# Twelve rows of each wo head on five DMA engines, instruction blocks aligned on three engines, x issued behind wq

## The chip, the cores and the metric

The kernel runs on one core of a Trainium2 chip. A core has TensorE (PE, with its weight loads as PEld), VectorE (DVE), ScalarE (ACT), GpSimd (POOL) and SyncE (SP), and 16 DMA engines. The metric is the device time of one execution in microseconds (us); lower is better.

## The reference

One decoding step of attention with grouped heads over a sliding window of the cache, with both projections. In bfloat16:

```python
B, Sq, D = 32, 1, 512
Hq, Hkv, Sk, Dh = 32, 8, 2048, 128
W = min(4096, max(256, Sk // 4))             # 512: the last 512 positions
rep = Hq // Hkv                              # 4
q = (x @ wq).reshape(B, Sq, Hq, Dh).transpose(0, 2, 1, 3)
k = repeat(k_cache[:, :, Sk - W:, :], rep, axis=1)
v = repeat(v_cache[:, :, Sk - W:, :], rep, axis=1)
p = softmax(einsum("bhqd,bhkd->bhqk", q, k) * Dh ** -0.5)
o = einsum("bhqk,bhkd->bhqd", p, v)
return o.transpose(0, 2, 1, 3).reshape(B, Sq, Hq * Dh) @ wo
```

wq is 512 x 4096 and wo 4096 x 512 (4 MB each); the windows of the two caches are 32 MB each.

## The kernel before

**Stages.** x (32 x 512) is transposed on PE by a selection matrix (L325), copied to SBUF by DVE (L453), and multiplied with wq (L336: 8 groups of 4 matmuls, copied out by DVE and ACT in turn). DVE transposes q to `QT_sb` (L483), and POOL builds from it the block-diagonal `QBD` (L312), one batch quarter at a time. Then come eight rounds q = 0 to 7 of four batch rows each, with these steps (a letter is a step in the written orders below):

- K, V (SP, L248 and L255): load the round's K and V rows, 4 MB each; later V's in two pieces;
- T (DVE, L491): transpose half of K into `KT_sb[:, w]`; S (PE, L353): scores of that half;
- M (DVE): maximum, X (ACT): exponential and sum, N (DVE): normalising;
- E (PE, L368): probabilities to the rows of V, with the selection matrices `E_sb`; G (ACT): copy out;
- B (DVE and ACT): spread over heads by a mask into `bd`; P (PE, L383): times V, 32 groups;
- C (DVE and ACT): pick the wanted blocks into `C_sb`;
- F and D (PE L395, ACT L561): fold the first 4 x NI values of each head with `F_sb` into `o_sel`; H and U (PE L404, ACT L566): fold the last NX values with `F_ext` into `o_ext`.

At the end PE multiplies with wo in three pieces W0, W1, W2 (L421) and with the extra rows (L435), two copies take the two halves out (DVE L524, ACT L582), and SP and ACT store them (L233).

**How wo is laid out.** A head has 128 rows of wo, 1 KB each. Rows 0 to 4 x NI - 1 go to 128 partitions (32 heads x 4 groups of NI rows), in pieces `WOP` of those NI rows (L269); NI is 30, so 120 rows of a head. The last NX = 128 - 4 NI = 8 rows of each head go to a tile of 64 partitions, one head on a partition, by four small loads, `HEADS` (L262). They reuse the memory of `QT_sb`, which ACT first fills with zeros (step Z0, L572, after POOL has made its last `QBD`).

**Orders.** Each compute engine runs a written list of steps (`PE_OPS`, `DVE_OPS`, `ACT_OPS`); `needs` says which other steps each waits for. SP issues the loads in the order of `LOADS`, waiting in order, so a load stands behind every load written ahead of it. x's three loads are issued by ACT (L204), wq by SP (L208), ahead of the rest. POOL builds constants at the start, among them the four shifted copies of `E_sb` (L301); DVE makes `F_sb` (L471) and `F_ext` (L474). `pe.addr_align(256, offset=178)` places PE's code: its next instruction is loaded 178 slots past a boundary of 256 instruction slots. The other engines' code is not placed.

Of the kernel before, what the change touches and what calls it, by code (L numbers as in the profile page):

```python
# [5 lines left out]
BF16 = mybir.dt.bfloat16  # L6
# [14 lines left out]
P2.12.32 F2 H2 S4.0 S4.1 P3.0.12 E4 P3.12.32 S5.0 S5.1 S6.0 P4.0.4 E5 P4.4.8 S6.1 P4.8.24 E6 P4.24.32  # L21
F3 H3 S7.0 P5.0.20 S7.1 P5.20.32 E7 F4 H4 P6.0.32 F5 H5 P7.0.32 F6 H6 F7 H7
"""
# [6 lines left out]
X0 X1 G0 B0.4.8 G1 B1.4.8 C0.0.4 D0 U0 X2 G2 B2.4.8 C1.0.4 D1 U1 X3 G3 B3.4.8 C2.0.4 D2 U2 X4 G4 B4.4.8  # L30
C3.0.2 X5 G5 B5.4.8 X6 G6 C4.0.2 B6.4.7 D3 U3 B6.7.8 Z0 X7 C5.0.2 G7 B7.5.6 D4 U4 B7.6.8 C6.0.2 D5 U5 C7.0.2
D6 U6 D7 U7
"""
# [6 lines left out]
V_PIECES = 5 * [[0, 32]] + 2 * [[0, 16, 32]] + [[0, 18, 32]]  # L40
WOP = [(0, 20), (20, 28), (28, 30)]
HEADS = [(0, 20, 4, 0), (20, 25, 1, 32), (25, 30, 1, 33), (30, 32, 1, 34)]
# [6 lines left out]
def bass_standalone__sliding_block_cached__sampling_kernel(  # L49
# [8 lines left out]
    B, Sq, D = x.shape  # L58
# [11 lines left out]
    R = W // KB  # L70
    NI = 30
    NX = DH - 4 * NI
# [57 lines left out]
    with ExitStack() as es:  # L130
# [17 lines left out]
        F_ext = sb("F_ext", [P, 64], F32)  # L148
        E_sb = sb("E_sb", [P, KB, REP, 32, KB], BF16)
        F_sb = sb("F_sb", [P, 4, HQ, 4], F32)  # L150
# [8 lines left out]
        wo_sb = K_sb[0][:, 0:NI * D].rearrange("p (i n) -> p i n", i=NI)  # L159
        wx_row = QT_sb[0:64].rearrange("p j w h t -> p (j w h t)")  # L160
        wx_sb = wx_row.rearrange("p (i n) -> p i n", i=NX)
# [17 lines left out]
        def folds(q):  # L179
# [10 lines left out]
            "pe_xT pe_q pe_Y dve_xT dve_q dve_QT dve_m dve_r dve_c act_q act_warm out_y "  # L190
            "pool_x pool_e pool_ei pool_q pool_f pool_m pool_j pool_qbd pool_fz"
        ).split()
# [9 lines left out]

        for b0, b1 in X_PARTS:
            nc.scalar.dma_start(  # L204
                x_sb[b0:b1, :], x[b0:b1].rearrange("b s d -> b (s d)")
            ).then_inc(sem_x, 16)

        nc.sync.dma_start(  # L208
            V_sb[1][:, :], wq.rearrange("(p k) n -> p (k n)", k=DKT)
        ).then_inc(sem_wq, 16)  # L210
        regions = es.enter_context(ExitStack())
        block = regions.enter_context(nc.Block())
# [25 lines left out]
        @block.sync  # L238
        def _(sp):
            wait = Waits(sp)  # L240
            wo_h = wo.rearrange("(h r) n -> h (r n)", r=DH)
            wo_r = wo_h[:, 0:4 * NI * D].rearrange("h (d m) -> h d m", d=4)
            for op in ops_of(" ".join(LOADS)):
                kind, q = op[0], op[1]
                if kind == "K":
                    if q >= 2:
                        wait([ends["T", q - 2, 1]])
                    sp.dma_start(K_sb[q % 2][:, :], rows(k_cache, q)).then_inc(sem_k[q % 2], 16)  # L248
                elif kind == "V":
                    if q == 1:  # L250
                        sp.wait_ge(s["pe_q"], 8)
                    r0, r1 = (4 * g for g in V_PIECES[q][op[2]:op[2] + 2])
                    if q >= 2:
                        wait([ends["P", q - 2, r1 // 4 - 1]])
                    sp.dma_start(  # L255
                        V_sb[q % 2][:, r0 * DH:r1 * DH], rows(v_cache, q, r0, r1)
                    ).then_inc(sem_v[q % 2][op[2]], 16)
                elif kind == "A":
                    wait([ends["Z", 0]])
                    h0, h1, k, p0 = HEADS[q]  # L260
                    n = (h1 - h0) // k
                    sp.dma_start(  # L262
                        wx_row[p0:p0 + 4 * n:1 if k == 4 else 4, :],
                        wo_h[h0:h1, 4 * NI * D:].rearrange("(k j) m -> j k m", k=k),
                    ).then_inc(sem_wx, 16)
                else:
                    wait([ends["T", NQ - 2, 1]])
                    i0, i1 = WOP[q]
                    sp.dma_start(  # L269
                        wo_sb[:, i0:i1, :].rearrange("p i n -> p (i n)"),  # L270
                        wo_r[:, :, i0 * D:i1 * D],
                    ).then_inc(sem_wo[q], 16)
            store(sp, 0)

        @block.gpsimd
        def _(pool):
            wait = Waits(pool)

            def diag(t, pattern, name):
# [16 lines left out]
                 [[-1, REP], [-4, 4], [-16, HKV]], "pool_ei")  # L296
            pool.memset(E_sb[:, :, :, :, :], 0.0).then_inc(s["pool_e"], 1)
            pool.wait_ge(s["pool_e"], 1)
            pool.wait_ge(s["pool_ei"], 2)
            for k in range(KB):  # L300
                pool.tensor_copy(E_sb[:, k, :, :, k], E_id[:, :, :]).then_inc(s["pool_e"], 1)  # L301
            pool.wait_ge(s["pool_e"], 5)
            pool.wait_ge(s["pool_q"], 1)
            pool.wait_ge(s["dve_QT"], 1)
            for q in range(NQ):
                if q >= 2:
                    wait([ends["S", q - 2, 1]])
                for b in range(4):
                    pr = slice(32 * b, 32 * b + 32)
                    if q or b:  # L310
# [4 lines left out]
                        QT_sb[pr, q].rearrange("p w (h e) t -> p w t h e", h=HKV),  # L315
                    ).then_inc(s["pool_qbd"], 1)

        @block.tensor
        def _(pe):
            pe.addr_align(256, offset=178)  # L320
            wait = Waits(pe)
# [41 lines left out]
            def to_value_rows(q):  # L363
                if q == 0:
                    pe.wait_ge(s["pool_e"], 5)
                for e in range(REP):
                    for k in range(KB):
                        ins = pe.matmul(  # L368
                            EP_ps[:, e * R:(e + 1) * R],
                            lhsT=E_sb[:, k, e].rearrange("p m j -> p (m j)"),  # L370
                            rhs=P_bf[:, k * R:(k + 1) * R],
                            start=k == 0, stop=k == KB - 1, tile_position=(0, 0),
                        )
                return ins
# [16 lines left out]
            def fold(q):  # L391
                if q == 0:
                    pe.wait_ge(s["dve_c"], 7 + len(HEADS))
                for d in range(4):
# [15 lines left out]
            for op in orders["PE"]:  # L410
                wait(needs(op))
                run[op[0]](*op[1:]).then_inc(op_sem["PE", op[0]], 1)
            wait([ends["D", NQ - 1]])
            for j, (i0, i1) in enumerate(WOP):
                pe.wait_ge(sem_wo[j], 16)
                last = j == len(WOP) - 1
                for cs in ((0, 1), (2, 3)) if last else (range(4),):
                    for i in range(i0, i1):
                        for c in cs:
                            n = 2 * (c % 2) + c // 2  # L420
                            ins = pe.matmul(  # L421
                                Y_ps[32 * c:32 * (c + 1), 0:P],
                                lhsT=o_sel[:, i, :],
                                rhs=wo_sb[:, i, n * P:(n + 1) * P],
                                start=i == 0, stop=i == NI - 1, tile_position=(0, 32 * c),
                            )
                    if last:
                        ins.then_inc(s["pe_Y"], 1)
                if j == 0:
                    wait([ends["U", NQ - 1]])  # L430
                    pe.wait_ge(sem_wx, 16 * len(HEADS))
                    for i in range(NX):
                        for c in range(4):
                            n = 2 * (c % 2) + c // 2
                            pe.matmul(  # L435
                                Y_ps[32 * c:32 * (c + 1), 0:P],
                                lhsT=o_ext[:, i, :],
                                rhs=wx_sb[:, i, n * P:(n + 1) * P],
                                start=False, stop=False, tile_position=(0, 32 * c),
                            )  # L440

# [8 lines left out]
        def _(dve):  # L450
# [14 lines left out]
            dve.wait_ge(s["dve_c"], 2)  # L465
            dve.wait_ge(s["pool_fz"], 2)
            dve.tensor_reduce(
                mask[:, :], m_red[:, :].rearrange("p (h k) -> p h k", h=HKV), AX.X, ALU.add
            ).then_inc(s["dve_c"], 1)
            for d in range(4):  # L470
                dve.tensor_copy(F_sb[:, d, :, d], F_hd[:, :]).then_inc(s["dve_c"], 1)  # L471
            for h0, h1, k, p0 in HEADS:
                n = (h1 - h0) // k
                dve.tensor_copy(  # L474
                    F_ext[:, p0:p0 + 4 * n].rearrange("p (j k) -> p k j", k=4)[:, 0:k],
                    F_hd[:, h0:h1].rearrange("p (k j) -> p k j", k=k),
                ).then_inc(s["dve_c"], 1)
            for n in range(4):
# [48 lines left out]
        def _(act):  # L527
# [41 lines left out]

            def zero(_):  # L570
                act.wait_ge(s["pool_qbd"], 4 * NQ)
                return act.activation(  # L572
                    wx_row, junk[0:64, 0:1].to_broadcast([64, NX * D]), ACTF.Copy
                )

            run = {"X": exponential, "G": gather, "B": spread, "C": pick, "D": folded,
                   "U": folded_ext, "Z": zero}
            for op in orders["ACT"]:
# [36 lines left out]
```

## Time and profile before

| | |
|---|---|
| median of 3 runs | 184.42 us (184.26 to 184.52) |
| the profiled execution | 184.59 us |
| its span, first to last instruction | 183.3 us |
| mean granted clock of TensorE | 0.842 |
| busy: PE, DVE, ACT, POOL | 120.4, 106.7, 54.2, 17.1 us |
| moved by DMA | 75.80 MB, mean 414 GB/s |

The profile is of one execution. Busy times are of one engine each and overlap. In the chain of waits a line "SPq" is SyncE issuing a transfer, and "DMA a<-b" the time from an issue to the landing that ended a wait. The landing of a transfer is that of its last DMA engine.

### The profile page before, as it was taken

To read this page: it belongs to the slowest core of one execution; us is meant where nothing else is said; L and a number is where in the kernel's file an instruction comes from. 1 tells how busy PE (TensorE), PEld (TensorE's weight loads), DVE (VectorE), ACT (ScalarE), POOL (GpSimd) and SP (SyncE) were. 2 spreads that over 40 slices of the span, in tenths; PEclk is the share of its full clock that TensorE was granted. 3 is DMA by queue.
4 is the path that set the end of the run, shared out by engine and by line. 5 is a ranking of instruction groups with operands and counts; after the bars stand their busy time and mean duration, and the time that the engine had idled before them with its cause. 6 is when DMAs were issued, how large, how long until landed. Compare 5 with 4: busy or idle time off the path is not lost.

```text
span 183.3 us, 3870 instructions
## 1 busy us (share of the span) xinstructions
PE 120.4 (66%) x1676; PEld 58.0 (32%) x1676; DVE 106.7 (58%) x109; ACT 54.2 (30%) x101; POOL 17.1 (9%) x53
## 2 busy tenths in 40 slices
PE   0029802416779699429944995440799978999984
PEld 0013300002535344304520252000255433655463
DVE  0042399998569534973289326999825994703030
ACT  3001300010590527501650135001053693803040
POOL 7900013020200020002000200001000000000000
PEclk9999995555769999996995599655559999999999
DMA  6998999989999999999999999999999999999981
GB/s 234 459 443 386 429 458 454 422 386 451 458 443 383 429 454 447 415 401 451 442 429 415 424 442 440 408 429 451 436 408 404 426 426 429 432 418 427 436 359 62
DMA packets 3517, 75.80 MB, mean 414 GB/s; under 512 B 429, under 2 KB 525, under 8 KB 653
## 3 DMA queue, kind: packets, MB, share of 16 engines
q1 hardware_dynamic: 3409, 75.52, 96.5%
q8 instruction: 13, 0.21, 0.5%
q10 hardware_dynamic: 92, 0.05, 0.1%
q14 instruction: 3, 0.02, 0.0%
HBM read 75.53 MB, written 0.03 MB: 412 GB/s over the span
## 4 chain that ended last, share of the span: by engine, by line
DMA 65%; DVE 19%; PE 8%; issue 4%; SPq 3%; ACT 0%; DVEq 0%
DMA K_sb<-in_k_cache_dram 32%; DVE KT_sb L491 16%; DMA V_sb<-in_v_cache_dram 16%; DMA K_sb<-in_wo_dram 11%; DMA V_sb<-in_wq_dram 7%; PE ps L336 5%; PE ps L383 2%; DVE QT_sb L483 2%; SPq L262 2%; SPq L255 1%; PE ps L421 1%; PE ps L353 1%; DVE C_sb L516 0%; SPq L269 0%; ACT KT_sb L533 0%
## 5 line engine op out<-in xcount | busy, mean ns | idle before, releaser
L491 DVE STREAM_TRANSPOSE KT_sb<-K_sb 128x4096 f32<-128x4096 f32 x16 | 70.5, 4430 | 7.2 <-DMA K_sb<-in_k_cache_dram 7.1
L383 PE MATMUL ps<-V_sb,bd 32*128 32x512 bf16 x1024 | 64.0, 402 | 4.4 <-DMA V_sb<-in_v_cache_dram 2.1
L353 PE MATMUL ps<-KT_sb,QBD 128*32 128x512 bf16 x256 | 24.7, 522 | 35.2 <-DVE KT_sb L491 26.0
L383 PEld LDWEIGHTS ps<-V_sb,bd 32*128 32x128 bf16 x1024 | 27.7, 98 | 37.8 <-issue 14.1
L353 PEld LDWEIGHTS ps<-KT_sb,QBD 128*32 128x32 bf16 x256 | 6.4, 111 | 50.4 <-DVE KT_sb L491 31.3
L539 ACT ACTIVATE P_f<-ps,negmax 128x512 f32<-128x512 f32 x8 | 5.5, 687 | 56.8 <-DVE negmax L499 56.8
L557 ACT ACTIVATE C_sb<-ps 32x512 f32<-32x512 f32 x22 | 12.9, 588 | 24.4 <-PE ps L383 24.2
L552 ACT ACTIVATE bd<-PTc,mask 128x512 bf16<-128x512 bf16 x31 | 20.1, 712 | 0.3
L312 POOL COPY QBD<-QT_sb 32x128 bf16<-32x128 bf16 x32 | 9.3, 289 | 106.3 <-PE ps L353 87.2
L511 DVE TENSOR_SCALAR bd<-PTc,mask 128x512 bf16<-128x512 bf16 x33 | 9.4, 349 | 14.0 <-ACT PTc L546 14.0
L516 DVE COPY C_sb<-ps 32x512 f32<-32x512 f32 x10 | 6.9, 693 | 13.9 <-PE ps L383 13.8
L395 PE MATMUL ps<-C_sb,F_sb 128*128 128x120 f32 x64 | 9.2, 286 | 6.8 <-ACT C_sb L557 6.5
L497 DVE TENSOR_REDUCE maxv<-ps 128x1 f32<-128x512 f32 x8 | 5.5, 687 | 10.8 <-PE ps L353 10.7
L395 PEld LDWEIGHTS ps<-C_sb,F_sb 128*128 128x128 f32 x64 | 7.7, 191 | 9.6 <-ACT C_sb L557 8.4
L368 PE MATMUL ps<-P_bf,E_sb 128*128 128x128 bf16 x128 | 9.9, 239 | 1.0 <-DVE P_bf L505 1.0
L336 PE MATMUL ps<-V_sb,bd 128*128 128x512 bf16 x32 | 9.0, 451 | 2.0 <-DMA V_sb<-in_wq_dram 2.0
L546 ACT ACTIVATE PTc<-ps 128x512 bf16<-128x512 f32 x8 | 4.7, 593 | 18.3 <-PE ps L368 18.3
L368 PEld LDWEIGHTS ps<-P_bf,E_sb 128*128 128x128 bf16 x128 | 8.4, 108 | 4.9 <-DVE P_bf L505 2.8
L325 PE MATMUL ps<-bd 32*128 32x128 bf16 x4 | 0.6, 298 | 10.5 <-DMA bd<-in_x_dram 10.5
L533 ACT ACTIVATE KT_sb<-ps 128x512 bf16<-128x512 f32 x4 | 2.4, 597 | 17.0 <-PE ps L336 17.0
L453 DVE CAST bd<-ps 128x512 bf16<-128x512 f32 x1 | 0.7, 692 | 11.2 <-PE ps L325 11.2
L480 DVE CAST KT_sb<-ps 128x512 bf16<-128x512 f32 x4 | 2.8, 692 | 6.0 <-PE ps L336 6.0
(37 smaller groups left out, 44.1 us busy)
## 6 DMA issues: line engine op xcount, KB each, us to landing
K_sb<-in_k_cache_dram SPq DMA_DIRECT2D x8, 4096.0 KB, 24.6
V_sb<-in_v_cache_dram SPq DMA_DIRECT2D x5, 4096.0 KB, 28.7
V_sb<-in_v_cache_dram SPq DMA_DIRECT2D x4, 2048.0 KB, 20.6
V_sb<-in_wq_dram SPq DMA_DIRECT2D x1, 4096.0 KB, 12.3
K_sb<-in_wo_dram SPq DMA_DIRECT2D x1, 2560.0 KB, 17.6
V_sb<-in_v_cache_dram SPq DMA_DIRECT2D x1, 2304.0 KB, 14.2
V_sb<-in_v_cache_dram SPq DMA_DIRECT2D x1, 1792.0 KB, 14.9
K_sb<-in_wo_dram SPq DMA_DIRECT2D x1, 1024.0 KB, 19.4
```

Source lines behind the costliest of these rows:

```text
L312: pool.tensor_copy(QBD[pr, q % 2].rearrange("p (w t) (h c) -> p w t h c", w=2, h=HKV)[:, :, :, :, 4 * b:4 * b + 4], QT_sb[pr, q].rearrange ...
L336: ins = pe.matmul(ps[:, n], lhsT=xT_sb[:, kt, :], rhs=wq_sb[:, kt, n * 512:(n + 1) * 512], start=kt == 0, stop=kt == DKT - 1, tile_positio ...
L353: ins = pe.matmul(S_ps[32 * c:32 * c + 32, :], lhsT=QBD[:, q % 2, 2 * w + t, c0:c0 + 32], rhs=KT_sb[:, w, :, KB * h:KB * h + KB, t], start ...
L368: ins = pe.matmul(EP_ps[:, e * R:(e + 1) * R], lhsT=E_sb[:, k, e].rearrange("p m j -> p (m j)"), rhs=P_bf[:, k * R:(k + 1) * R], start=k = ...
L383: ins = pe.matmul(O_ps[:, b, :], lhsT=bd[pr, q % 2, 4 * g:4 * g + 4].rearrange("p r h e -> p (r h e)"), rhs=V_sb[q % 2][pr, 512 * g:512 * ...
L395: ins = pe.matmul(folds(q), lhsT=F_sb[:, d].rearrange("p h d -> p (h d)"), rhs=C_sb[:, q % 2, :, NI * d:NI * d + NI], start=d == 0, stop=d ...
L491: return dve.transpose(KT_sb[:, w].bitcast(F32).rearrange("p r c t -> p r (c t)"), K_sb[q % 2][:, :].bitcast(F32).rearrange("p (r w c) -> ...
L497: dve.tensor_reduce(maxv[:, q:q + 1], S_ps, AX.X, ALU.max).then_inc(s["dve_m"], 1)
L511: ins = dve.tensor_scalar(o, i, m, None, op0=ALU.mult)
L516: ins = dve.tensor_copy(*pick_args(q, r))
L552: ins = act.activation(o, i, ACTF.Copy, scale=m)
L557: ins = act.activation(*pick_args(q, r), ACTF.Copy)
```

## The change

1. NI goes from 30 to 29: wo's three pieces hold 19, 8 and 2 rows instead of 20, 8 and 2, and each head's last 12 rows, instead of 8, go by the four small loads. Their tile moves from `QT_sb` to the memory of `KT_sb[0:64, 0]`; POOL zeroes it after S7.0, in place of ACT's Z0.
2. DVE, ACT and POOL get `addr_align(128, offset=0, max_nops=0)` ahead of their work; PE's offset goes from 178 to 154.
3. x's three loads are issued by SP behind wq, not by ACT.
4. Small work moves: the copies to `F_sb` and `F_ext` go from DVE to POOL; `E_sb` becomes one padded matrix for each of the four heads of a group, of which E takes a shifted window, so three of its four copies go.
5. At the end the extra rows' matmuls come first, ahead of W0; H7 comes ahead of F7, U6 ahead of D6 and U7 ahead of D7.

```diff
--- before.py
+++ after.py
@@ -19,7 +19,7 @@
 PE_OPS = """
 S0.0 S0.1 S1.0 S1.1 E0 E1 P0.0.32 S2.0 F0 H0 S2.1 P1.0.12 E2 P1.12.32 F1 H1 S3.0 S3.1 P2.0.12 E3
 P2.12.32 F2 H2 S4.0 S4.1 P3.0.12 E4 P3.12.32 S5.0 S5.1 S6.0 P4.0.4 E5 P4.4.8 S6.1 P4.8.24 E6 P4.24.32
-F3 H3 S7.0 P5.0.20 S7.1 P5.20.32 E7 F4 H4 P6.0.32 F5 H5 P7.0.32 F6 H6 F7 H7
+F3 H3 S7.0 P5.0.20 S7.1 P5.20.32 E7 F4 H4 P6.0.32 F5 H5 P7.0.32 F6 H6 H7 F7
 """
 DVE_OPS = """
 T0.0 T0.1 T1.0 M0 T1.1 N0 M1 N1 B0.0.4 B1.0.4 T2.0 T2.1 M2 N2 B2.0.4 T3.0 T3.1 M3 N3 B3.0.4 T4.0
@@ -28,8 +28,8 @@
 """
 ACT_OPS = """
 X0 X1 G0 B0.4.8 G1 B1.4.8 C0.0.4 D0 U0 X2 G2 B2.4.8 C1.0.4 D1 U1 X3 G3 B3.4.8 C2.0.4 D2 U2 X4 G4 B4.4.8
-C3.0.2 X5 G5 B5.4.8 X6 G6 C4.0.2 B6.4.7 D3 U3 B6.7.8 Z0 X7 C5.0.2 G7 B7.5.6 D4 U4 B7.6.8 C6.0.2 D5 U5 C7.0.2
-D6 U6 D7 U7
+C3.0.2 X5 G5 B5.4.8 X6 G6 C4.0.2 B6.4.7 D3 U3 B6.7.8 X7 C5.0.2 G7 B7.5.6 D4 U4 B7.6.8 C6.0.2 D5 U5 C7.0.2
+U6 D6 U7 D7
 """
 
 LOADS = """
@@ -38,7 +38,7 @@
 
 X_PARTS = [(0, 25), (25, 30), (30, 32)]
 V_PIECES = 5 * [[0, 32]] + 2 * [[0, 16, 32]] + [[0, 18, 32]]
-WOP = [(0, 20), (20, 28), (28, 30)]
+WOP = [(0, 19), (19, 27), (27, 29)]
 HEADS = [(0, 20, 4, 0), (20, 25, 1, 32), (25, 30, 1, 33), (30, 32, 1, 34)]
 
 
@@ -68,7 +68,7 @@
     NQ = B // 4
     KB = 4
     R = W // KB
-    NI = 30
+    NI = 29
     NX = DH - 4 * NI
     NG = 4
 
@@ -146,7 +146,7 @@
         o_sel = sb("o_sel", [P, NI, B], BF16)
         o_ext = sb("o_ext", [64, NX, B], BF16)
         F_ext = sb("F_ext", [P, 64], F32)
-        E_sb = sb("E_sb", [P, KB, REP, 32, KB], BF16)
+        E_sb = sb("E_sb", [P, REP, 33, KB], BF16)
         F_sb = sb("F_sb", [P, 4, HQ, 4], F32)
         mask = sb("mask", [P, HKV], F32)
         maxv = sb("maxv", [P, NQ], F32)
@@ -157,7 +157,7 @@
 
         wq_sb = V_sb[1][:, :].rearrange("p (kt n) -> p kt n", kt=DKT)
         wo_sb = K_sb[0][:, 0:NI * D].rearrange("p (i n) -> p i n", i=NI)
-        wx_row = QT_sb[0:64].rearrange("p j w h t -> p (j w h t)")
+        wx_row = KT_sb[0:64, 0].rearrange("p r c t -> p (r c t)")[:, 0:NX * D]
         wx_sb = wx_row.rearrange("p (i n) -> p i n", i=NX)
 
 
@@ -188,7 +188,7 @@
         sem_out = sem("sem_out")
         names = (
             "pe_xT pe_q pe_Y dve_xT dve_q dve_QT dve_m dve_r dve_c act_q act_warm out_y "
-            "pool_x pool_e pool_ei pool_q pool_f pool_m pool_j pool_qbd pool_fz"
+            "pool_x pool_e pool_ei pool_q pool_f pool_m pool_j pool_qbd pool_fz pool_z"
         ).split()
         s = {n: sem(n) for n in names}
         op_sem = {key: sem("op_%s_%s" % key) for key in total}
@@ -200,14 +200,16 @@
                     c = sum(1 for p in range(q % 2, q + 1, 2) if len(V_PIECES[p]) > i + 1)
                     yield g, sem_v[q % 2][i], 16 * c
 
-        for b0, b1 in X_PARTS:
-            nc.scalar.dma_start(
-                x_sb[b0:b1, :], x[b0:b1].rearrange("b s d -> b (s d)")
-            ).then_inc(sem_x, 16)
+        for eng in (nc.vector, nc.scalar, nc.gpsimd):
+            eng.addr_align(128, offset=0, max_nops=0)
 
         nc.sync.dma_start(
             V_sb[1][:, :], wq.rearrange("(p k) n -> p (k n)", k=DKT)
         ).then_inc(sem_wq, 16)
+        for b0, b1 in X_PARTS:
+            nc.sync.dma_start(
+                x_sb[b0:b1, :], x[b0:b1].rearrange("b s d -> b (s d)")
+            ).then_inc(sem_x, 16)
         regions = es.enter_context(ExitStack())
         block = regions.enter_context(nc.Block())
 
@@ -256,7 +258,7 @@
                         V_sb[q % 2][:, r0 * DH:r1 * DH], rows(v_cache, q, r0, r1)
                     ).then_inc(sem_v[q % 2][op[2]], 16)
                 elif kind == "A":
-                    wait([ends["Z", 0]])
+                    sp.wait_ge(s["pool_z"], 1)
                     h0, h1, k, p0 = HEADS[q]
                     n = (h1 - h0) // k
                     sp.dma_start(
@@ -294,12 +296,21 @@
 
             diag(E_id[:, :, :].rearrange("p e (b h) -> p e b h", b=4),
                  [[-1, REP], [-4, 4], [-16, HKV]], "pool_ei")
-            pool.memset(E_sb[:, :, :, :, :], 0.0).then_inc(s["pool_e"], 1)
+            pool.memset(E_sb[:, :, :, :], 0.0).then_inc(s["pool_e"], 1)
             pool.wait_ge(s["pool_e"], 1)
             pool.wait_ge(s["pool_ei"], 2)
-            for k in range(KB):
-                pool.tensor_copy(E_sb[:, k, :, :, k], E_id[:, :, :]).then_inc(s["pool_e"], 1)
-            pool.wait_ge(s["pool_e"], 5)
+            pool.tensor_copy(E_sb[:, :, 0:32, KB - 1], E_id[:, :, :]).then_inc(s["pool_e"], 1)
+            pool.wait_ge(s["pool_e"], 2)
+            pool.wait_ge(s["pool_fz"], 2)
+            pool.wait_ge(s["dve_c"], 1)
+            for d in range(4):
+                pool.tensor_copy(F_sb[:, d, :, d], F_hd[:, :]).then_inc(s["pool_fz"], 1)
+            for h0, h1, k, p0 in HEADS:
+                n = (h1 - h0) // k
+                pool.tensor_copy(
+                    F_ext[:, p0:p0 + 4 * n].rearrange("p (j k) -> p k j", k=4)[:, 0:k],
+                    F_hd[:, h0:h1].rearrange("p (k j) -> p k j", k=k),
+                ).then_inc(s["pool_fz"], 1)
             pool.wait_ge(s["pool_q"], 1)
             pool.wait_ge(s["dve_QT"], 1)
             for q in range(NQ):
@@ -314,10 +325,12 @@
                             :, :, :, :, 4 * b:4 * b + 4],
                         QT_sb[pr, q].rearrange("p w (h e) t -> p w t h e", h=HKV),
                     ).then_inc(s["pool_qbd"], 1)
+            wait([ends["S", NQ - 1, 0]])
+            pool.memset(wx_row, 0.0).then_inc(s["pool_z"], 1)
 
         @block.tensor
         def _(pe):
-            pe.addr_align(256, offset=178)
+            pe.addr_align(256, offset=154)
             wait = Waits(pe)
             pe.wait_ge(s["pool_x"], 2)
             pe.wait_ge(sem_x, 16 * len(X_PARTS))
@@ -362,12 +375,13 @@
 
             def to_value_rows(q):
                 if q == 0:
-                    pe.wait_ge(s["pool_e"], 5)
+                    pe.wait_ge(s["pool_e"], 2)
                 for e in range(REP):
+                    window = E_sb[:, e].rearrange("p m j -> p (m j)")
                     for k in range(KB):
                         ins = pe.matmul(
                             EP_ps[:, e * R:(e + 1) * R],
-                            lhsT=E_sb[:, k, e].rearrange("p m j -> p (m j)"),
+                            lhsT=window[:, KB - 1 - k:KB - 1 - k + P],
                             rhs=P_bf[:, k * R:(k + 1) * R],
                             start=k == 0, stop=k == KB - 1, tile_position=(0, 0),
                         )
@@ -390,7 +404,7 @@
 
             def fold(q):
                 if q == 0:
-                    pe.wait_ge(s["dve_c"], 7 + len(HEADS))
+                    pe.wait_ge(s["pool_fz"], 6 + len(HEADS))
                 for d in range(4):
                     ins = pe.matmul(
                         folds(q),
@@ -410,34 +424,30 @@
             for op in orders["PE"]:
                 wait(needs(op))
                 run[op[0]](*op[1:]).then_inc(op_sem["PE", op[0]], 1)
+            wait([ends["U", NQ - 1]])
+            pe.wait_ge(sem_wx, 16 * len(HEADS))
+
+            def projected(lhsT, rhs, cs, first=False, last=False):
+                for c in cs:
+                    n = 2 * (c % 2) + c // 2
+                    ins = pe.matmul(
+                        Y_ps[32 * c:32 * (c + 1), 0:P],
+                        lhsT=lhsT, rhs=rhs[:, n * P:(n + 1) * P],
+                        start=first, stop=last, tile_position=(0, 32 * c),
+                    )
+                return ins
+
+            for i in range(NX):
+                projected(o_ext[:, i, :], wx_sb[:, i], range(4), first=i == 0)
             wait([ends["D", NQ - 1]])
             for j, (i0, i1) in enumerate(WOP):
                 pe.wait_ge(sem_wo[j], 16)
                 last = j == len(WOP) - 1
                 for cs in ((0, 1), (2, 3)) if last else (range(4),):
                     for i in range(i0, i1):
-                        for c in cs:
-                            n = 2 * (c % 2) + c // 2
-                            ins = pe.matmul(
-                                Y_ps[32 * c:32 * (c + 1), 0:P],
-                                lhsT=o_sel[:, i, :],
-                                rhs=wo_sb[:, i, n * P:(n + 1) * P],
-                                start=i == 0, stop=i == NI - 1, tile_position=(0, 32 * c),
-                            )
+                        ins = projected(o_sel[:, i, :], wo_sb[:, i], cs, last=i == NI - 1)
                     if last:
                         ins.then_inc(s["pe_Y"], 1)
-                if j == 0:
-                    wait([ends["U", NQ - 1]])
-                    pe.wait_ge(sem_wx, 16 * len(HEADS))
-                    for i in range(NX):
-                        for c in range(4):
-                            n = 2 * (c % 2) + c // 2
-                            pe.matmul(
-                                Y_ps[32 * c:32 * (c + 1), 0:P],
-                                lhsT=o_ext[:, i, :],
-                                rhs=wx_sb[:, i, n * P:(n + 1) * P],
-                                start=False, stop=False, tile_position=(0, 32 * c),
-                            )
 
         def spread_args(q, h):
             return bd[:, q % 2, :, h, :], PTc[:, q % NG], mask[:, h:h + 1]
@@ -463,18 +473,9 @@
                 m_id[:, :, :, :].rearrange("p b h k -> p h k b"), AX.X, ALU.add,
             ).then_inc(s["dve_c"], 1)
             dve.wait_ge(s["dve_c"], 2)
-            dve.wait_ge(s["pool_fz"], 2)
             dve.tensor_reduce(
                 mask[:, :], m_red[:, :].rearrange("p (h k) -> p h k", h=HKV), AX.X, ALU.add
             ).then_inc(s["dve_c"], 1)
-            for d in range(4):
-                dve.tensor_copy(F_sb[:, d, :, d], F_hd[:, :]).then_inc(s["dve_c"], 1)
-            for h0, h1, k, p0 in HEADS:
-                n = (h1 - h0) // k
-                dve.tensor_copy(
-                    F_ext[:, p0:p0 + 4 * n].rearrange("p (j k) -> p k j", k=4)[:, 0:k],
-                    F_hd[:, h0:h1].rearrange("p (k j) -> p k j", k=k),
-                ).then_inc(s["dve_c"], 1)
             for n in range(4):
                 dve.wait_ge(s["pe_q"], 2 * n + 1)
                 dve.tensor_copy(Q_row[:, 1024 * n:1024 * n + 512], ps[:, 2 * n]).then_inc(s["dve_q"], 1)
@@ -567,14 +568,8 @@
                     o_ext[:, :, 4 * q:4 * q + 4],
                     EP_ps[0:64, 0:4 * NX].rearrange("p (b i) -> p i b", b=4), ACTF.Copy)
 
-            def zero(_):
-                act.wait_ge(s["pool_qbd"], 4 * NQ)
-                return act.activation(
-                    wx_row, junk[0:64, 0:1].to_broadcast([64, NX * D]), ACTF.Copy
-                )
-
             run = {"X": exponential, "G": gather, "B": spread, "C": pick, "D": folded,
-                   "U": folded_ext, "Z": zero}
+                   "U": folded_ext}
             for op in orders["ACT"]:
                 wait(needs(op))
                 run[op[0]](*op[1:]).then_inc(op_sem["ACT", op[0]], 1)
```

## The prediction

> **What bounds the kernel now.** I read the page first, for the DMA row and the queues.
>
> ```profile
> span 183.3 us, 3870 instructions
> DMA  6998999989999999999999999999999999999981
> q1 hardware_dynamic: 3409, 75.52, 96.5%
> q8 instruction: 13, 0.21, 0.5%
> q14 instruction: 3, 0.02, 0.0%
> ```
>
> The 16 DMA engines are full from the second slice to the last but one, nearly all of it SyncE's queue (q1); no compute engine passes 66%. Two small queues matter: 13 instruction fetches of 16 KB (q8) and 3 of 8 KB (q14) share those engines. Next the chain of waits at its end:
>
> ```profile
> 156.52 0.54 SPq L255
> ...
> 160.21 0.61 SPq L269
> ...
> 160.86 19.41 DMA K_sb<-in_wo_dram
> 180.27 0.04 issue
> 180.32 1.00 PE ps L421 x40
> 181.31 0.02 issue
> 181.34 0.27 ACT P_bf L582
> ```
>
> The end is set by wo's landing. Its three pieces are issued by 162.1 and land at 177.83, 180.27 and 180.90 (trace); then come 8 matmuls, two copies and the stores, 2.37 us to the end of the span. So the question is when the slowest DMA engine finishes. The windows show the engines finish unevenly (last two columns: share of the 16 engines, GB/s):
>
> ```profile
> 168.00:175.00 7.00, 7.00 (x128) 3.51 (x121) 0.32 (x1) 0.32 (x1) 0.00 (x0) 1.00 1.02 433
> 175.00:177.00 2.00, 1.71 (x16) 1.52 (x15) 1.07 (x2) 1.20 (x4) 0.00 (x0) 1.00 0.89 371
> 177.00:178.00 1.00, 0.62 (x10) 0.42 (x12) 0.00 (x0) 0.42 (x2) 0.00 (x0) 1.00 0.84 348
> 178.00:179.00 1.00, 1.00 (x76) 1.00 (x80) 0.00 (x0) 0.00 (x0) 0.00 (x0) 1.00 0.64 262
> 179.00:180.00 1.00, 0.82 (x52) 0.54 (x40) 0.00 (x0) 0.00 (x0) 0.00 (x0) 1.00 0.46 168
> ```
>
> From 175 on engines run dry. The lost share, 0.11x2 + 0.16 + 0.36 + 0.54 and 0.46 in the last half microsecond, is 1.7 us of all engines: the most that perfect levelling could bring, before any other bound.
>
> Packets of one engine follow each other without a gap, so the trace's packet records (start, length, size) can be chained into 16 engines. The last packet ends at:
> - three engines with neither fetches nor the 8 KB rows of L262: 176.85, 177.09, 177.32;
> - four that served one 16 KB fetch: 178.49 to 178.63;
> - four that served two: 180.01, 180.09, 180.16, 180.48, the last of these the latest of all; its semaphore lands 0.42 later, at 180.90;
> - five that carry the L262 rows (that semaphore gets 5+5+5+2 landings): 178.87 to 180.02.
>
> Ahead of L262 the first group had ended V7.1 at 167.62 to 168.09, the single-fetch group at 169.28 to 169.43: a 16 KB fetch (record: 1.0 to 1.1 us) sets its engine back 1.4 to 1.5 us for good. The five ended V7.1 at 167.77, 168.00, 168.41, 168.49, 168.94. The three late ones are those that served the 8 KB fetches at 87.65, 100.83 and 108.06 (records 0.31 to 0.33 us; set back 0.6, 0.6 and 1.0).
>
> **The change, part by part.** I sum against the profiled execution (184.59 us, span 183.27), 0.17 above the median of the runs; differences are then laid on the median, 184.42.
>
> *NI 30 to 29.* Every engine moves 29 rows of wo instead of 30. The stretch from V7.1 to the end took 9.22 us for 30 rows (167.62 to 176.85), so a row is 0.31. The eleven engines without extras save that. On the lowest five, packets of L262 grow from 8 to 12 KB; records have 0.309 for 8 KB, 0.611 for 16 KB, so 0.46 for 12. An engine has 6 of them (two have 7): from 1.85 or 2.16 to 2.76 or 3.22, less 0.31: net +0.60 or +0.75.
>
> *Aligned blocks.* If the three 8 KB fetches leave the middle of the stream, three of the five are 0.6 to 1.0 earlier; if they stay, nothing. The trace does not show the aligned case. PE's alignment is the nearest row: at offset 178 its first boundary falls 78 instructions in; the first fetch (31.6) comes as the first score matmuls start (31.06), after 72 matmuls and loads. So a fetch follows the crossing of a boundary. 256 slots go with 16 KB, so 128 with 8 KB. The trace has 133 rows on DVE, 121 on ACT, 74 on POOL, sequencer rows included. The diff takes 8 copies and a wait from DVE (124 left), three DMA issues, Z0 and a wait from ACT, and brings POOL to some 85: each fits one 128-slot block, and a block entered at its first slot is crossed at the start, before wq's first packet (1.80). I take the three fetches as gone, and keep the other end for a rival. PE's offset 154 moves each crossing 24 slots later, and 24 instructions are added, so all its fetches remain, each under 1 us later; the 13th now falls some 30 instructions into W0, near 179, on an engine of the second group that is done by 178.3. Cost nothing.
>
> The Trainium skill (Runtime: NRT & Kernel Launch, section Instruction fetch mechanics) says that crossing a block boundary costs one DMA tail-bump, mostly hidden. That speaks against this part; by it the sum would lack the gain of the aligned blocks and would be that of the first rival. The 1.4 us between the first two groups disagrees for the DMA stream.
>
> *x behind wq.* x's packets go on the same five engines, 6 or 7 of 0.046 us: 0.3 at most if they now stand in the full stream, nothing if they cost as much before, when half ran at 1.7 to 2.2 ahead of wq and the rest at 6 to 10 within it. I take +0.15. wq's first packets started at 1.80 to 2.73; without x ahead of them, 0 to 0.2 earlier for all; I take 0.1. x now lands with wq, near 13.3 instead of 10.4:
>
> ```profile
> 10.54 0.58 PE L325 MATMUL ps<-bd 32*128 32x128 bf16 x4 [10.54 <-DMA bd<-in_x_dram]
> 11.17 0.69 DVE L453 CAST bd<-ps 128x512 bf16<-128x512 f32 x1 [11.17 <-PE ps L325]
> 13.17 9.01 PE L336 MATMUL ps<-V_sb,bd 128*128 128x512 bf16 x32 [2.04 <-DMA V_sb<-in_wq_dram]
> ```
>
> These 1.5 us of transposing x now follow wq's landing: the projection starts 1.7 late, and so do the first transposes and the issues of K2 (35.36 to 37.1) and V1. The queue holds V0 until 41.7, so 4.6 us of cover are left; from T2 on DVE waits for K's landing and the delay is gone. On SyncE the three x issues (0.26 to 0.58 each on ACT) push K0, K1 and V0 back by 1.1, behind wq's 10 us of transfer. Without that cover it would cost 1.7.
>
> *Moved small work.* F_sb and F_ext copies go to POOL, which then idles until QT (26.5); needed first by F0, after 60. Three copies to E_sb go. Zeroing wx (3.60 us on ACT, 148.2 to 151.8) becomes a POOL memset of 6144 elements; by L289's row (2048 in 1.80) 5.4 us, from S7.0's end (146.4) to 151.8. L262 is issued at 157.1, and its engines are busy with V7.1 until 168. All at nothing.
>
> *Tail on PE.* L435 grows from 32 to 48 matmuls (0.63 to 0.95) and now precedes W0, which falls from 80 to 76 (1.24). F7 ends near 177.6, so both end near 179.8; W1 lands at 180.27 now, some 0.3 sooner after. No cost, but a ceiling: a stream over 0.5 us faster meets PE.
>
> **Sum.** Two-fetch engines: 180.48 - 0.31 = 180.17. The five: 168.00 (their latest without an 8 KB fetch) + 0.15 + 2.76 or 3.22 + 8.91 = 179.8 or 180.3. The last end moves from 180.48 to 180.3, 0.2 earlier, 0.3 with the earlier start: 184.42 - 0.3 = 184.1. The bound passes from the two-fetch engines to the two that carry seven rows.
>
> **The rivals.** *The 8 KB fetches stay, or are not what held those three back.* For it: no row shows what an aligned start fetches. Against: three fetches, three late engines. Then the five end at up to 180.02 + 0.60 = 180.62 and 179.88 + 0.75 = 180.63, with x's 0.15 180.78: +0.3, 184.7 (184.5 to 184.9, as x's price is 0 to 0.3). It decides once two or more of the three remain. Slower. 18 in 100.
>
> *A larger gain.* The two-fetch engine at 180.48 lies 0.32 behind its three fellows; if that was this execution's chance, if x costs the five nothing and the start gains 0.2, the end is 180.15 - 0.2 = 179.95, and the gain 0.5, where PE's tail meets it: 183.85. 20 in 100.
>
> *The late x leaves the stream dry.* It would need K2 issued after V0's 41.7, so 6.4 us of delay where I count 1.7; each further microsecond is one of time, some 185.5 for one. 4 in 100.
>
> **How the numbers follow.** My forecast keeps 58 in 100, at 184.1 (183.9 to 184.3 alone). A measurement of this kernel can tell some 0.2%, 0.37 us, so faster means under 184.05 and slower over 184.79. Two fifths of the forecast lie under 184.05 (0.23); with the larger gain 0.43. The first rival splits about its 184.7; as the spread above it is the wider I give 0.16 of its 0.18 to slower, and all 0.04 of the dry stream: 0.20. The rest, 0.37, is the same. The range runs from 183.7, under the larger gain, to 184.85, over the first rival.
>
> **What would show it.** Right: q14 has no fetch between 5 and 170 us; wo's last landing near 180.6 with the five's and the two-fetch engines' ends within 0.3 of each other; the DMA share in 178 to 180 higher, in 180 to 180.5 near nothing; the projection starts near 14.9 and K2's issue near 37, with no dip in the DMA row by 42. Wrong: 8 KB fetches still in mid-stream, a wait of PE on L262's semaphore or on D7 at the end, POOL's memset past 157.

## The result

The changed kernel takes 185.18 us, median of 6 runs (185.09 to 185.41), against 184.45 for 6 runs of the kernel before (184.26 to 184.57): ratio 1.0040, 95% interval 1.0029 to 1.0051. It is slower by 0.73 us. Its profiled execution took 185.09 us, span 183.8. One execution of a later kernel, the one with only x moved, took 206.07 us at a granted clock of 0.65 (0.81 to 0.85 in the others) and is left out of its time.

The page after, its DMA row and its queues:

```profile
span 183.8 us, 3870 instructions
DMA  6999999999999999999999999999999999999981
q1 hardware_dynamic: 3453, 75.55, 96.3%
q8 instruction: 13, 0.21, 0.5%
q14 instruction: 3, 0.02, 0.1%
```

The stream is as full as before, and none of the fetches is gone: 13 of 16 KB, 3 of 8 KB. What moved is where the three stand. The DMA view of 1 to 8 us, which held none before:

```profile
q1 hardware_dynamic: 79, 2.59, 94.3%
q14 instruction: 3, 0.02, 2.1%
```

The packet records put them at 1.74, 1.83 and 3.69 us. x's transpose, the projection with wq and the issue of K2 come later than before (start, length, what):

```profile
14.56 0.58 PE L338 MATMUL ps<-bd 32*128 32x128 bf16 x4 [14.56 <-DMA bd<-in_x_dram]
15.93 8.62 PE L349 MATMUL ps<-V_sb,bd 128*128 128x512 bf16 x32 [0.79 <-DVE bd L463]
37.73 0.54 SPq L250 DMA_DIRECT2D K_sb<-in_k_cache_dram  x1
```

The end of the chain of waits (start, length, what):

```profile
160.89 19.91 DMA K_sb<-in_wo_dram
180.80 0.04 issue
180.85 0.63 PE ps L433 x32
181.48 0.00 issue
181.48 0.37 PE ps L433 x8
```

As before, PE waits for wo's second piece, and what follows is the same work: the second piece lands at 180.80 instead of 180.27 and the third at 181.44 instead of 180.90. The windows show who is still moving at the end (last two columns: share of the 16 engines, GB/s):

```profile
178.00:179.00 1.00, 1.00 (x80) 0.90 (x69) 0.00 (x0) 0.15 (x1) 0.00 (x0) 1.00 0.62 258
179.00:180.00 1.00, 0.80 (x60) 0.62 (x47) 0.00 (x0) 0.00 (x0) 0.00 (x0) 1.00 0.54 203
180.00:180.50 0.50, 0.00 (x0) 0.00 (x0) 0.00 (x0) 0.00 (x0) 0.00 (x0) 1.00 0.19 74
```

From 180 to 180.5 there is twice the share of before, whose line was:

```profile
180.00:180.50 0.50, 0.18 (x14) 0.18 (x17) 0.00 (x0) 0.00 (x0) 0.00 (x0) 1.00 0.09 33
```

A share of 0.19 is the work of three engines, 0.09 that of one and a half: more engines end late. The trace's landings (each DMA engine's own) say which. Ordered, the last five of wo's third piece are 180.54, 180.62, 180.66, 181.04, 181.44. The extra rows' semaphore gives the five engines that carry these rows: the first load, four heads on each engine, lands 1.85 us after V7.1 on every one, so it identifies their V7.1 landings as 168.37, 168.52, 168.94, 169.00 and 169.78. Adding six or seven packets of 0.46 and 29 rows (8.91, the prediction's figure) to these gives 180.0, 180.7, 181.1, 180.7 and 181.4: the two last landings are engines of the five. The engines with two 16 KB fetches, last before, are among those that land by about 180.6.

Three engines are late from the start: K0, the first load behind wq, lands at 23.04, 23.10 and 23.87 on three engines and by 22.81 on the others, where before the latest was 22.72. The three latest of the five V7.1 landings, 168.94, 169.00 and 169.78, have the same steps between them.

### The profile page after: what moved, and what is told of

It reads as the page before. It is cut to its first block, busy times and chain, and to the rows that moved or that the text cites. A ratio compares the mean times of both kernels' runs of the same rounds, so it can differ in the third digit from the quotient of the medians.

```text
span 183.8 us, 3870 instructions
## 1 busy us (share of the span) xinstructions
PE 118.2 (64%) x1688; PEld 58.3 (32%) x1688; DVE 106.4 (58%) x101; ACT 50.8 (28%) x100; POOL 21.1 (12%) x59
## 4 chain that ended last, share of the span: by engine, by line
DMA 50%; PE 19%; DVE 19%; issue 6%; SPq 3%; ACT 2%; DVEq 0%
DMA K_sb<-in_k_cache_dram 16%; DMA V_sb<-in_v_cache_dram 16%; DVE KT_sb L492 15%; DMA K_sb<-in_wo_dram 11%; PE ps L397 8%; DMA bd<-in_x_dram 7%; PE ps L349 5%; PE ps L382 3%; PE ps L366 2%; DVE QT_sb L484 2%; SPq L264 2%; ACT C_sb L558 1%; PE ps L409 1%; DVE bd L512 1%; SPq L257 1%
## 5 line engine op out<-in xcount | busy, mean ns | idle before, releaser
L397 PE MATMUL ps<-V_sb,bd 32*128 32x512 bf16 x1024 | 61.1, 388 | 3.8 <-DMA V_sb<-in_v_cache_dram 2.6
L397 PEld LDWEIGHTS ps<-V_sb,bd 32*128 32x128 bf16 x1024 | 27.0, 95 | 35.2 <-issue 10.1
L409 PE MATMUL ps<-C_sb,F_sb 128*128 128x116 f32 x64 | 9.3, 287 | 6.5 <-ACT C_sb L558 6.5
L382 PE MATMUL ps<-P_bf,E_sb 128*128 128x128 bf16 x128 | 11.0, 253 | 0.8 <-DVE P_bf L506 0.8
L382 PEld LDWEIGHTS ps<-P_bf,E_sb 128*128 128x128 bf16 x128 | 9.4, 115 | 4.9 <-DVE P_bf L506 3.2
L329 POOL MEMSET KT_sb<- 64x6144 bf16 x1 | 5.2, 5211 | 21.8 <-PE ps L366 21.8
## 6 DMA issues: line engine op xcount, KB each, us to landing
V_sb<-in_v_cache_dram SPq DMA_DIRECT2D x1, 1792.0 KB, 14.9
```

Source lines behind the costliest of these rows:

```text
L382: ins = pe.matmul(EP_ps[:, e * R:(e + 1) * R], lhsT=window[:, KB - 1 - k:KB - 1 - k + P], rhs=P_bf[:, k * R:(k + 1) * R], start=k == 0, st ...
L397: ins = pe.matmul(O_ps[:, b, :], lhsT=bd[pr, q % 2, 4 * g:4 * g + 4].rearrange("p r h e -> p (r h e)"), rhs=V_sb[q % 2][pr, 512 * g:512 * ...
L409: ins = pe.matmul(folds(q), lhsT=F_sb[:, d].rearrange("p h d -> p (h d)"), rhs=C_sb[:, q % 2, :, NI * d:NI * d + NI], start=d == 0, stop=d ...
```

## The experiments

Three theories were tested. One: the five engines carry the end, because the 8 KB fetches were moved and not removed, and the 12 KB rows come on top. Two: x behind wq costs. Three: the aligned starts cost by themselves. Times below are medians, with the ratio to the kernel before on the same chip and its 95% interval.

**Undoing one part at a time.** Rows back to 8:

```diff
-WOP = [(0, 19), (19, 27), (27, 29)]
+WOP = [(0, 20), (20, 28), (28, 30)]
-    NI = 29
+    NI = 30
-            pe.addr_align(256, offset=154)
+            pe.addr_align(256, offset=178)
```

> The changed kernel with the rows undone: NI 30, 8 rows of a head on the five engines (PE offset 178 again). Theory one, the five engines carry the end (their 8 KB fetches were moved to the start of the stream, not removed, and still set them back 0.5 to 1.0 us; the 12 KB rows come on top): the last landing of wo falls from 181.44 to about 180.9, the time from 185.2 to 184.6. Theory two, x behind wq (projection at 15.9 instead of 13.2) is what costs: the time stays near 185.1. Theory three, the aligned starts themselves cost: it stays near 185.1.

184.86 us, 1.0025 (1.0009 to 1.0041). In the profiled execution (184.58) the last landing is 180.83, as theory one expects; the twelve executions spread from 184.51 to 185.93, and the longer ones have no trace. Half of the loss is left, so the rows are not all.

The aligned starts taken out:

```diff
-        for eng in (nc.vector, nc.scalar, nc.gpsimd):
-            eng.addr_align(128, offset=0, max_nops=0)
```

> The changed kernel without the three aligned starts. Theory one: the 8 KB fetches go back to mid-stream with set-backs of 0.6, 0.6 and 1.0, so the five end about as late as now: last landing 181.2 to 181.4, time 184.9 to 185.2. Theory two (late x): 185.2. Theory three (alignment costs by itself): 184.5.

185.32 us, 1.0050 (1.0034 to 1.0067). The fetches are back at 87.8, 89.2 and 108.7, and the last landing is 181.60. Time and landing are both a little above what theory one gave, and nothing is gained: theory three falls.

x ahead of wq again, by ScalarE, behind its aligned start:

```diff
+        for b0, b1 in X_PARTS:
+            nc.scalar.dma_start(x_sb[b0:b1, :], ...)
         nc.sync.dma_start(V_sb[1][:, :], wq...)
-        for b0, b1 in X_PARTS:
-            nc.sync.dma_start(x_sb[b0:b1, :], ...)
```

> The changed kernel with x issued by ScalarE ahead of wq again. Theory one: x's share of the five engines' time is at most 0.3 us, so 184.9 to 185.2; the projection starts near 13.2 again, and K2's issue near 35.4, without effect on the end. Theory two (the late x is the cause): 184.5, last landing near 180.9. Theory three: 185.2.

187.01 us, 1.0137 (1.0113 to 1.0162): a miss for all three theories. The timeline (start, length, what; x's issue, x's transpose, the issue of K2):

```profile
1.18 3.14 ACTq L207 DMA_DIRECT2D bd<-in_x_dram  x3
18.09 0.58 PE L339 MATMUL ps<-bd 32*128 32x128 bf16 x4 [18.09 <-DMA bd<-in_x_dram]
42.08 0.54 SPq L251 DMA_DIRECT2D K_sb<-in_k_cache_dram  x1
```

Right behind an aligned start, ScalarE's three issues took 3.14 us (the first alone 2.48) and ended at 4.31, where before they were done at 1.92. x landed at 17.95, and K2 was issued at 42.08, with V0, the last load queued, landing from 41.7 on. The windows show the stream running dry:

```profile
38.00:42.00 4.00, 1.68 (x16) 0.30 (x8) 4.00 (x2) 0.00 (x0) 0.00 (x0) 0.50 0.74 315
42.00:44.00 2.00, 1.89 (x16) 0.44 (x16) 2.00 (x2) 0.00 (x0) 0.00 (x0) 0.50 0.92 246
44.00:46.00 2.00, 0.01 (x2) 0.00 (x0) 2.00 (x1) 0.00 (x0) 1.14 (x4) 0.50 0.65 279
```

V2's first landing is 83.26 instead of 80.60, and the whole run is 2.5 us longer. This is the prediction's third rival, in a kernel that was not meant to show it. Its price was too low: K2 came 0.4 us after the first landing of V0, and K2's mean landing fell 2.4 us further behind V0's (table below), where the rival took one microsecond for each further one. The changed kernel's profile, with K2 at 37.73, stays clear of it.

**One part alone.** The rows, with the moved small work (no aligned starts, x ahead of wq):

> The rows alone, with the moved small work: NI 29, no aligned starts, x by ScalarE ahead of wq. Theory one: the five engines of the kernel before, plus 0.60 or 0.75: last packet near 181.0 instead of 180.5, time 184.8 to 185.0. Theories two and three: the kernel before's time, 184.4, or 0.1 below.

184.90 us, 1.0024 (1.0014 to 1.0034). The last landings are 180.92 and 181.17, both of the five: their V7.1 landings, 168.80 and 169.50, with seven and six packets of 0.46 and the 8.91 give 180.9 and 181.2. The last packet ends at 180.7, 0.3 sooner than expected, but the time is as expected. Theory one holds for this part.

Rows and aligned starts, with x's issues ahead of ScalarE's aligned start:

> Rows and aligned starts, x ahead of wq (ScalarE's aligned start stands behind its x issues, so x is not held up). The prediction's step (aligned starts take the three 8 KB fetches off the stream): 184.1. Theory one (the fetches only move to the stream's first microseconds and set their engines back all the same): 184.9, as the rows alone.

184.90 us, 1.0023 (1.0014 to 1.0032): the aligned starts are worth nothing. This kernel differs from the changed one in x's place alone, and that is the step from 1.0023 to 1.0040. Its DMA view of 1 to 8 us has the three fetches (records at 1.73, 3.88 and 6.49):

```profile
q14 instruction: 3, 0.02, 1.2%
```

In the rows alone they stand at 88.68, 88.84 and 100.68. The mean landing over the 16 engines shows the same loss early in one kernel and late in the other:

| | K0 | V2 | V3 | K5 | V7.1 |
|---|---|---|---|---|---|
| the rows alone | 22.44 | 81.11 | 100.76 | 110.61 | 169.56 |
| rows and aligned starts | 22.60 | 81.26 | 100.79 | 110.60 | 169.56 |

The 0.15 us of the mean engine are 2.4 us of engine time, 0.8 for each fetch.

x behind wq, with 8 rows, no aligned starts, and the moved small work; and then the same with x in one load over all 16 engines (`X_PARTS = [(0, 32)]`):

> x behind wq alone, with the moved small work: 8 rows (NI 30), no aligned starts. Theory one (only the five engines' bytes count; x adds at most 0.3 us to engines that end 0.5 before the last): 184.4 to 184.6. Theory two (the projection that starts 2 to 3 us late costs by itself): 184.8 to 185.0, the same gap that the two kernels with 12 rows showed (185.3 against 184.9).

> As the last, but x's 32 rows in one load over all 16 engines, two rows on each. If x's packets on the five are what costs: back to 184.5. If the late projection costs: as the last one, 184.8 to 185.0, since the projection starts no sooner.

184.80 us, 1.0017 (1.0007 to 1.0027), and 184.78, 1.0017 (1.0008 to 1.0025). Spreading x changes nothing, so it is not its share of the five engines' time. Both of these kernels hold the moved small work as well; the last two runs part them, the small work alone and the place of x alone:

> The moved small work and the order of the tail alone: 8 rows (NI 30), x ahead of wq, no aligned starts. If the 0.3 us of the kernel with x behind wq comes from x: 184.45, the kernel before's time, mean landing of K0 22.45. If it comes from the small work or the order: 184.8.

> The kernel before with x issued by SyncE behind wq and nothing else changed. If x's place costs through the stream (K0's mean landing near 22.7 instead of 22.46): 184.7 to 184.9. If only the small work or the order costs: 184.45.

184.55 us, 1.0008 (1.0000 to 1.0017), and 184.76, 1.0018 (1.0008 to 1.0028). It is x's place (and its issue by SyncE, which moved with it); the small work may cost 0.1, at the edge of its interval. The mean landing over the 16 engines shows when the time is lost (the row "x behind wq" is the kernel with the small work):

| | wq | K0 | V7.1 |
|---|---|---|---|
| before | 12.75 | 22.46 | 169.54 |
| small work alone | 12.78 | 22.49 | 169.56 |
| x behind wq | 12.78 | 22.75 | 169.87 |
| x behind wq, over 16 engines | 12.79 | 22.66 | 169.85 |
| the changed kernel | 12.77 | 22.70 | 169.65 |

wq lands no sooner without x ahead of it. K0 lands 9.87 to 9.98 after wq on the mean engine in all seven profiles with x behind wq (9.90 with nothing but x moved, where K0's landing of 22.60 falls short of the 22.7 expected), and 9.70 to 9.74 in the nine with x ahead. With 8 rows and no aligned starts the loss is still there at V7.1. In the changed kernel some 0.1 of it is: its three 8 KB fetches are paid by K0, those of the kernel before at 88 to 108, so the lead of the latter falls from 0.26 at V2 to 0.11 at K5. x's 32 packets of 0.046 are 0.09 of the 0.2 to 0.3, spread over 16 engines; by the packet records K0's own packets took 9.74 to 9.82 us an engine instead of 9.70 in the three kernels with 8 rows and no aligned starts. Why those are longer is open, and another 0.03 to 0.06 is in no record's length.

The later projection has a share of its own in some executions. It delays K2, and the mean landing of K2 behind that of V0, the load ahead of it in the queue, shows when the delay reaches the stream:

| | projection lasts | K2 issued | K2 behind V0 |
|---|---|---|---|
| before | 9.01 | 35.36 | 9.71 |
| the changed kernel | 8.62 | 37.73 | 9.71 |
| its rows back to 8 | 9.16 | 38.28 | 9.84 |
| its rows on eight engines (below) | 9.97 | 39.06 | 10.09 |
| x ahead, behind the aligned start | 9.43 | 42.08 | 12.10 |

So the cover ends near 38, some 4 us before V0's first landing at 41.7, and the changed kernel's profiled execution has little of it left. Whether this makes the longer executions of these kernels is not shown, as they have no trace.

**Other engines for the extra rows.** One load of 32 heads goes to eight engines, four heads on each (A1 to A3 leave `LOADS`):

```diff
-HEADS = [(0, 20, 4, 0), (20, 25, 1, 32), (25, 30, 1, 33), (30, 32, 1, 34)]
+HEADS = [(0, 32, 4, 0)]
```

This was put into the changed kernel, into the rows alone with 12 and with 16 rows (NI 28), and into the kernel before with its 8:

> The changed kernel with the 12 rows of each head in one load over eight engines (four heads on each) instead of four loads over five (six or seven heads). Theory one (the five carry the end): an engine's extra packets fall from 2.76 or 3.22 us to 1.85, the last landing goes from 181.44 to about 180.6, set by engines with two 16 KB fetches; time 184.3 to 184.5. If the extra rows are not what ends last, 185.2.

> The rows alone (no aligned starts, x ahead of wq), 12 rows of each head over eight engines. Theory one: extras end by 180.2, the two-fetch engines by 180.2 to 180.6 (landings), 0.3 below the kernel before: 184.1 to 184.3. Otherwise no better than the rows alone over five, 184.9.

> As the last, but with 16 rows of each head over eight engines and NI 28. Theory one: two-fetch engines by 179.9 to 180.3, extras by 180.5 at most; time 183.9 to 184.2, the lowest of all if PE's tail (projection of wo done near 180) leaves room. If PE's tail or something else ends last: 184.3 or more.

> The kernel before with its 8 rows of each head over eight engines instead of five, NI 30. Theory one: in the kernel before the two-fetch engines end last and the five just behind them, so the time stays within 0.2 of 184.45. If the five ended last before too: 0.5 or more lower.

186.08 (1.0089), 184.55 (1.0024), 186.00 (1.0064) and 185.32 us (1.0034): by the median none came out as theory one gave. Save in the changed kernel (185.33 to 186.63), the executions fall into two groups: with 12 rows, 8 at 184.18 to 184.75 and 4 at 185.67 to 186.11; with 16 rows, 3 below 185 and 9 from 185.95; in the kernel before, 4 up to 184.84 and 8 from 185.25.

The profile of the last is of its longer group: seven of the eight engines land their four extra packets between 169.44 and 170.86, the eighth at 172.45, and it ends alone at 181.59, the next one at 180.64. Less these packets (1.23), it landed V7.1 at 171.2, in the group of engines that served two 16 KB fetches; its chained packets hold those at 32.66 and 146.51. The profiles with 12 and 16 rows are of the shorter groups, and there the eight landed V7.1 by 169.8 and 169.9: none of them had served two. So the eight engines include some that serve PE's fetches. In the chained packets PE's 13 fetches go round eight engines nearly in turn, so that by the end five engines have served two, and two of the round's engines are among those with the extra rows. These two stand at different places of the round: first and eighth in the profile of the kernel before with its 8 rows, fifth and sixth in that with 16. That this place also differs between executions of one kernel is inferred from the groups; no kernel has a profile of both.

In the changed kernel's profile (185.33, its shortest execution) theory one does not hold: the last landings, 181.53 and 181.69, are not of the eight, of which the latest lands its extra packets at 172.10 and ends at 181.0. This is the execution of the table above that lost 0.4 at K2.

With six engines, in the kernel of the rows alone:

```diff
+HEADS = [(0, 24, 4, 0), (24, 30, 1, 32), (30, 32, 1, 33)]
```

> The rows alone, 12 of each head, over six engines instead of five (five or six heads on an engine): extras 2.31 us (2.77 on two) instead of 2.76 (3.22). Theory one, with six engines that serve no 16 KB fetch: last landing 180.5 to 180.7, time 184.2 to 184.5, below the rows over five (184.9). If the sixth engine serves 16 KB fetches: single executions near 186, as with eight engines.

185.38 us, 1.0058 (1.0029 to 1.0087): 6 executions at 184.48 to 184.70, 6 at 186.07 to 186.72. This is the expectation's second case: by the groups, already the sixth engine serves 16 KB fetches. The one profile is of the shorter group and does not show it. No version's median is below that of the kernel before.

## Why the prediction was wrong

Its forecast was 184.1, with the three 8 KB fetches gone from the stream. That step failed: they were moved and cost the same, so the first rival happened, with its sign and its mechanism, at 185.2 instead of 184.7, and x's place cost 0.3 where the sum had nearly nothing. Point by point:

- *What bounds the kernel*: right. In every profile but the one of x alone, the time is 3.64 to 3.77 us more than the last landing of wo, and in the kernels before, after and with the rows alone that landing was followed back to the bytes and fetches of single engines.
- *NI 30 to 29*: right in its terms. The two-fetch engines came sooner (by about 180.6 instead of 180.90), the packets of 12 KB cost 0.46 each, and the five ended last. The rows by themselves cost 0.3 (1.0024 against 1.0008 without them).
- *Aligned blocks*: the step that failed first. "A block entered at its first slot is crossed at the start, before wq's first packet" was wrong by a small time: the fetches stand at 1.74, 1.83 and 3.69, within the first wq packets, and one engine's wq lands at 13.95 with the others by 13.00. The sum took 0.6 to 1.0 off three engines; measured is nothing (1.0023 with, 1.0024 without the aligned starts), as time lost at an engine's first packets stood in its last landing as much as time lost later. The sign given for this step, no fetch between 5 and 170 us, came true and could not tell a fetch saved from a fetch moved. Three of the five carry V7.1 landings 0.5, 0.6 and 1.3 behind the mean of the other two, about the 0.6, 0.6 and 1.0 of before. By the rule of the Trainium skill (Runtime: NRT & Kernel Launch, section Instruction fetch mechanics), that the cost of a crossing is mostly hidden, this part gains nothing, as measured. Its reason is not what the traces show: these crossings are not hidden from the DMA stream, they were only moved.
- *x behind wq*: the second. The sum took +0.15 on five engines and -0.1 for all; it was about +0.2 for all at K0 and 0.3 in time. x ahead of wq was free: wq's mean landing is 12.75 with it and 12.77 without, and 25 of its 32 packets, not half, had run by 2.3. The projection started at 15.93 instead of the forecast 14.9, as x landed at 14.42, behind the fetch at 3.69; without the aligned starts it started at 14.96. In the profiled execution it kept its cover, with no dip by 42, but the cover was smaller than the 4.6 us of the prediction: it ends near 38, not at 41.7.
- *Moved small work*: put at nothing; 0.1 measured (1.0008, 1.0000 to 1.0017), which is not clear of noise.
- *Tail on PE*: right. The product with W0 ended at 179.81, as forecast, and PE then waited for wo.

The parts measured alone are 0.3 for the rows, 0.3 for x's place, 0.1 for the small work and 0 for the aligned starts: 0.7 of the 0.73. Each is known to some 0.1 to 0.2, so the sum is no finer than that. The rival's price was short by x's part. The second rival's own terms give 183.9, not its 183.85, which changes nothing here.

## What to carry to other kernels

In this kernel all DMA engines are full from start to end, and the time is that of the most loaded one. Everything that it serves counted alike, early or late: rows, small loads and instruction fetches. Moving a fetch did not save it (1.0023 against 1.0024); look where it lands before its room is given to other data. A small load cost nothing ahead of the stream and 0.3 us behind its first large load. A load that keeps the queue filled has to be issued well before the queue runs dry: here the margin was some 4 us.

## What the hardware showed

- Chained packets show that one 16 KB instruction fetch (1.0 to 1.1 us) sets its DMA engine back by 1.4 to 1.5 us for the rest of the run. By chains and landings an 8 KB fetch (0.31 to 0.9 us) sets it back by 0.5 to 1.3, at the start of the stream as in its middle.
- Up to V7.1, PE's fetches did not touch the five engines that carry the extra rows in the profiles of before, of after and of the rows alone; with rows on six or eight engines, executions of one kernel fell into groups whose medians lie 0.8 to 1.8 us apart.
- Issues by ScalarE right behind its aligned start took 3.14 us for three, against 1.19 without it.
- Loads of 4 MB that follow one another landed 9.7 us apart on the mean engine; issued 3.5 us before, 2.8 us before and 0.4 us after the first landing of the load ahead, the next one landed 9.84, 10.09 and 12.10 us behind it.
